# Longer rows for the tiles that hold the softplus's two halves

## The chip, the cores and the metric

One core of a Trainium2 chip runs the whole program. The metric is the time of one execution on the device, in microseconds. Before the change it is 933.11 us, the median of three runs (931.77 to 933.13).

## The reference

Three stages follow each other: a recurrence over time with complex decay (attention), a feed-forward network with softplus, and a gated one without a nonlinearity.

```python
# attention, per batch and head; a is scaled to a magnitude of at most 0.999
S_re, S_im = a_re*S_re - a_im*S_im + outer(k_t, v_t), a_re*S_im + a_im*S_re
y_t = q_t @ S_re                                    # 4 x 8 heads, 768 steps, 48 wide
x = y as (3072 tokens, 384)
h = x @ w_in;  g = max(h, 0) + log1p(exp(-abs(h)))  # 384 -> 2048, softplus
x = g @ w_out                                       # 2048 -> 384
out = ((x @ w1) * (x @ w2)) @ w3 @ w_out2           # 384 -> 1024 -> 1024 -> 384
```

## The kernel before

Attention is worked in 24 chunks of 128 steps: cumulative products of the decays by a scan on VectorE (tiles P and tm), then matmuls on scaled queries and keys (tiles qkp, pk, rs, sc, am, kT, S, yp). The first network takes the 3072 tokens in blocks: 128 and 256 tokens in plain float32 (tiles x, s, g, w), then seven blocks of 384. Those seven use pairs of float32r tiles, a rounded high half and the rest as a low half, and three products: high by high, low weight by high, high weight by low. For every group of 128 of the 2048 hidden columns (16 groups, index f) the function s1 makes nine matmuls into a PSUM tile s (weights ww..h and ww..l, moving operand xh or xl), three activations on ScalarE and one VectorE operation give the softplus g, ScalarE rounds it into gh (line 946), and VectorE subtracts, gl = g - gh (line 947). The function s2a then makes nine matmuls into three accumulators acc (moving operand gh or gl). The second network follows in six blocks of 512 tokens and eight groups: s3 makes 18 matmuls into pa and pb (moving operand in the tiles called bx: for even blocks in the slots of tag P, named bxh and bxl, for odd blocks in wb6 and wb7, shown as bx), VectorE and ScalarE make the product bg and its halves bgg (in the slots of xh and xl), and s2b makes nine matmuls into acc with the weights bwp.

On chip memory is laid out by pools, one behind the other in each of the 128 partitions, and in a pool by tag, in the order of first use; every tag has some slots, each one row long. Pool cp: identity and mask (512 bytes a row) and six small tiles. Pool wp: the weights, rows of 3072 or 6144 bytes. Pool sp: gh and gl (five slots of 1536 bytes each), e (two), xl and xh (two of 4608 each) and g (three of 1536). Pool ap: rs0, rs1 (8192), kT (3584), a, nt (3072), P (two of 6144), n2, tm, qk, qkp, v (480 floats, 1920 bytes), am, S and y. The first two gh slots hold ext at the start, two slots of gl hold pick: constants for attention, cleared by POOL (lines 576 to 583) and, for pick, filled from the identity by ten copies.

The order of all instructions is planned by the program itself: operations are recorded with prices (line 162 for POOL: `return 160 + n * 2.08, 200`, with n the elements a partition), and the method flush lists them by priority in 16 rounds, a backward and a forward pass each, of which the second adds random noise to the priorities (line 336); the round with the earliest end is kept. Operations that one wait links are found by 64-element cells of tiles. All DMAs are issued from SP's queue. Every recorded operation is shown with line 205, since there it is called.

Of the kernel before, what the change touches and what calls it, by code (L numbers as in the profile page):

```python
# [11 lines left out]
F32 = mybir.dt.float32  # L12
F32R = mybir.dt.float32r
# [9 lines left out]
P = 128  # L23
# [11 lines left out]
NB = 384  # L35

BLOCKS = [(0, 128), (128, 256)] + [(NB * i, NB) for i in range(1, NT // NB)]
NATIVE = 2
QKB = 1
GB = 3  # L40
HB = 5
# [319 lines left out]
def fused(ctx: ExitStack, tc: tile.TileContext, a_in, qk_in, v_in, wio, w12, w3t, wo2, q, k, v, a_re, a_im, outT):  # L361
# [18 lines left out]
    sp = fast.enter_context(tc.tile_pool(name="sp", bufs=2))  # L380
# [42 lines left out]
    def pst(tag, bufs, shape, name):  # L423
        return ps.tile(shape, F32, tag=tag, bufs=bufs, name=name)
# [29 lines left out]
    def norm(u):  # L454
# [27 lines left out]
        def s4():  # L482
# [9 lines left out]
            )  # L492

        return [s1, s2, s3, s4]

    def cmul(R, L):
# [68 lines left out]
    def qkp(u, i, f):  # L565
        V.tensor_tensor(
            out=c[u]["qkp"][:, :, :, i],
            in0=half(u),
            in1=gt(f).unsqueeze(1).to_broadcast([P, 2, G, T]),
            op=ALU.mult,  # L570
        )
# [1 line left out]
    def vcols(h):  # L573
        return slice(h * 64, h * 64 + D) if h < 6 else slice(384 + (h - 6) * D, 384 + (h - 5) * D)

    ext = [sp.tile([P, NB], F32, tag="gh", bufs=HB, name=f"ext{i}") for i in range(2)]
    for t in ext:
        GP.memset(t, 0.0)
    ext = [t.rearrange("p (r k n) -> p r k n", r=2, k=KC) for t in ext]
    picks = [sp.tile([P, NB], F32, tag="gl", bufs=HB, name=f"pick{i}") for i in range(2)]  # L580
    sels = {}
    for i in range(2):
        GP.memset(picks[i], 0.0)
    for h in range(H):
        for g in range(h * D // P, ((h + 1) * D - 1) // P + 1):
            p0 = max(h * D, g * P)
            n = min((h + 1) * D, (g + 1) * P) - p0
            i, c0 = divmod(len(sels) * 64, NB)
# [11 lines left out]
    def inv(u):  # L600
# [14 lines left out]
        def s3():  # L615
            s["qkp"] = ap.tile([P, 2, G, 2, T], F32, tag="qkp", bufs=QKB, name=f"qkp{u}")
            qkp(u, 0, s["qk"][:, 0])
# [35 lines left out]
        if u < PICK:  # L653
            return [s1, s2, s3, lambda: pick(0), s4, s5, lambda: pick(1)]
        return [s1, s2, s3, s4, s5, s6]

    def mm(u):
# [88 lines left out]
        def x():  # L746
            bi, c0 = block_of(u)
            if c0 == 0:
                if bi < NATIVE:
                    xt[bi] = (sp.tile([P, KC, NB], F32, tag="xh", bufs=XB, name=f"x{bi}"), None)  # L750
# [5 lines left out]
            xh, xl = xt[bi]  # L756
            if bi < NATIVE:
                A.copy(xh[:, :, d], s["y"][:, 0:KC])
# [18 lines left out]
    for us in groups:  # L777
        n = len(us)
# [131 lines left out]
    def w_split(f):  # L910
        ww[f] = w_tiles(f, f"ww{f}")
        split(ww[f][0], ww[f][1], w32[f])
# [3 lines left out]
    def s1(bi, f):  # L916
        _, n = BLOCKS[bi]
        native = bi < NATIVE
        if bi == NATIVE:
            w_split(f)  # L920
        xh, xl = xt[bi]
        pt = pst("s1", S1B, [P, NB], f"s1_{bi}_{f}")
        o = pt[:, 0:n]
        if native:
            prods = [(w32[f], xh)]
        else:
            prods = [(ww[f][0], xh), (ww[f][1], xh), (ww[f][0], xl)]
        i = 0
        for w, xx in prods:
            for k in range(KC):  # L930
                PE.matmul(
                    o, w[:, k * P : (k + 1) * P], xx[:, k, 0:n],
                    start=(i == 0), stop=(i == len(prods) * KC - 1),
                )
                i += 1
        e = sp.tile([P, NB], F32, tag="e", name=f"e_{bi}_{f}")[:, 0:n]
        A.activation(out=e, in_=o, func=AF.Abs)
        A.activation(out=e, in_=e, func=AF.Exp, scale=-1.0)
        A.activation(out=e, in_=e, func=AF.Ln, bias=1.0)
        g = sp.tile([P, NB], F32, tag="g", bufs=GB, name=f"g_{bi}_{f}")[:, 0:n]  # L940
        V.scalar_tensor_tensor(out=g, in0=o, scalar=0.0, in1=e, op0=ALU.max, op1=ALU.add)
        if native:
            return g, None
        gh = sp.tile([P, NB], F32R, tag="gh", bufs=HB, name=f"gh_{bi}_{f}")[:, 0:n]
        gl = sp.tile([P, NB], F32R, tag="gl", bufs=HB, name=f"gl_{bi}_{f}")[:, 0:n]
        A.copy(gh, g)
        V.tensor_tensor(out=gl, in0=g, in1=gh.bitcast(F32), op=ALU.subtract)
        return gh, gl
# [12 lines left out]
    def s2a(bi, f, gg):  # L961
        _, n = BLOCKS[bi]
        gh, gl = gg
        if bi < NATIVE:
            prods = [(w32[f][:, DM:], gh)]
# [58 lines left out]
    for bi in range(nblk):  # L1024
        last = bi == nblk - 1
        t0, n = BLOCKS[bi]
# [89 lines left out]
    for bi in range(NBB):  # L1116
        gq = {}
        for f in range(FB):
# [6 lines left out]
            while ncheck[0] < min(NCK, NCK * it // nit):  # L1125
                src, n = cks[ncheck[0]]
# [11 lines left out]
    for src, lim, op in (  # L1138
# [5 lines left out]
        n = src.shape[1]  # L1144
# [249 lines left out]
```

## Time and profile before

| | |
|---|---|
| median of three runs | 933.11 us |
| profiled execution | 932.9 us |
| its span, first to last instruction | 931.2 us |
| TensorE, matmuls busy | 905.4 us, 97% |
| VectorE busy | 727.6 us, 78% |
| ScalarE busy | 540.6 us, 58% |
| POOL busy | 12.2 us, 1% |
| mean granted TensorE clock | 0.998 |

Times in the profile count from the first instruction. Busy is the time in which an engine has an instruction; a matmul's duration overlaps with the next one's, so what a matmul costs is the distance between two starts. A plain float32 matmul has two records, a float32r matmul one. The names are those of the program, out<-in, buffer numbers left out; of a matmul's two inputs the first is the moving operand, the second the weights.

### The profile page before, as it was taken

Reading aid. Unit: us, or ns where it says so; the run is one execution under the profiler, and the core shown is the slowest. Engines: PE = TensorE matmul, PEld = TensorE weight load, DVE = VectorE, ACT = ScalarE, POOL = GpSimd, SP = SyncE. Lnnn points to the kernel's source line nnn. Section 1 sums busy time; section 2 is a strip of 40 time slices with the busy share of each in tenths; the row PEclk is TensorE's granted clock in tenths of the full one; section 3 lists DMA queues with packets and bytes.
Section 4 is the critical chain, followed back from the end, with each engine's and each line's share of the span. In section 5 each row is a group of like instructions: output and inputs, shape, how many; then the busy total and the mean of one; then the engine's idle time right before and its main releaser. Section 6 shows DMA issues by size and latency. Waiting matters only on the chain.

```text
span 931.2 us, 16377 instructions
## 1 busy us (share of the span) xinstructions
PE 905.4 (97%) x6081; PEld 815.5 (88%) x6081; DVE 727.6 (78%) x1591; ACT 540.6 (58%) x1111; POOL 12.2 (1%) x29
## 2 busy tenths in 40 slices
PE   3999999999999999999999999999999999999997
PEld 2579988899999999999999999998888888888885
DVE  6999999999999899999989855599888785231221
ACT  6679986478597688778676755773231323131212
POOL 5000000000000000000000000000000000000000
PEclk9999999999999999999999999999999999999999
DMA  9898218375444737363746255248888873000001
GB/s 341 302 329 311 67 49 197 94 161 132 124 116 115 191 65 183 86 167 62 204 117 154 77 135 140 68 145 247 248 261 246 255 239 120 1 34 0 35 1 38
DMA packets 81641, 136.38 MB, mean 146 GB/s; under 512 B 7504, under 2 KB 53136, under 8 KB 81552
## 3 DMA queue, kind: packets, MB, share of 16 engines
q1 hardware_dynamic: 81552, 135.25, 50.4%
q8 instruction: 49, 0.80, 0.4%
q14 instruction: 40, 0.33, 0.1%
HBM read 107.59 MB, written 26.74 MB: 144 GB/s over the span
## 4 chain that ended last, share of the span: by engine, by line
PE 81%; DVE 11%; DMA 4%; issue 1%; ACT 1%; SPq 1%; DVEq 0%; ACTq 0%
PE acc L205 28%; PE s L205 17%; PE pb L205 11%; PE pa L205 11%; PE yp L205 4%; PE wpa L205 3%; PE sc L205 3%; DVE tm L205 3%; DVE P L205 3%; DMA a<-a_in 2%; PE stp L205 1%; PE pk L205 1%; PE ktp L205 1%; DVE g L205 1%; DVE qkp L205 1%
## 5 line engine op out<-in xcount | busy, mean ns | idle before, releaser
L205 DVE TENSOR_TENSOR tm<-P 128x90 f32<-128x90 f32 (+3 forms) x240 | 145.9, 619 | 1.3
L205 ACT ACTIVATE e<-e 128x384 f32<-128x384 f32 (+2 forms) x288 | 134.6, 487 | 2.2
L205 DVE TENSOR_TENSOR bg<-pa,bg 128x512 f32<-128x512 f32 x48 | 33.1, 689 | 92.6 <-PE pa L205 82.3
L205 ACT ACTIVATE e<-s 128x384 f32<-128x384 f32 (+2 forms) x144 | 64.7, 452 | 59.6 <-PE s L205 51.4
L205 ACT CAST bgg<-bg 128x512 fp32r<-128x512 f32 x48 | 29.8, 621 | 104.2 <-DVE bg L205 104.2
L205 DVE SCALAR_TENSOR_TENSOR g<-s,e 128x384 f32<-128x384 f32 (+2 forms) x144 | 73.4, 514 | 17.4 <-ACT e L205 16.3
L205 DVE TENSOR_TENSOR P<-tm 128x45 f32<-128x45 f32 (+11 forms) x304 | 85.7, 345 | 1.0
L205 ACT COPY bg<-pb 128x512 f32<-128x512 f32 x48 | 28.2, 588 | 88.0 <-PE pb L205 79.3
L205 ACT CAST gh<-g 128x384 fp32r<-128x384 f32 x112 | 56.6, 507 | 17.2 <-DVE g L205 15.0
L205 DVE TENSOR_TENSOR gl<-g,gh 128x384 fp32r<-128x384 f32 x112 | 61.7, 557 | 5.2 <-ACT gh L205 4.9
L205 PE MATMUL wpa<-wo,w 128*128 128x384 f32 x128 | 44.6, 509 | 14.2 <-DVE w L205 14.2
L205 DVE CUSTOM_DVE_ANT_0 ck<-ckr 128x384 f32<-128x384 f32 x80 | 43.4, 543 | 16.2 <-DMA ckr<-w3t 7.0
L205 PE MATMUL sc<-rs 112*128 112x128 f32 x384 | 52.2, 276 | 0.7 <-DVE am L205 0.6
L205 PEld LDWEIGHTS wpa<-wo,w 128*128 128x128 f32 x128 | 25.2, 200 | 31.6 <-DVE w L205 14.1
L205 PEld LDWEIGHTS sc<-rs 112*128 112x128 f32 x384 | 49.6, 191 | 2.7 <-DVE g L205 0.9
L205 PE MATMUL acc<-bgg,bwp0h 128*128 128x512 f32 x144 | 50.4, 389 | 0.0
L205 PE MATMUL acc<-bgg,bwp2h 128*128 128x512 f32 x144 | 48.7, 389 | 0.0
L205 DVE TENSOR_TENSOR bgg<-bg,bgg 128x512 fp32r<-128x512 f32 x48 | 33.0, 688 | 15.8 <-ACT bgg L205 15.8
L205 DVE TENSOR_REDUCE lims<-ck 128x1 f32<-128x384 f32 x80 | 43.1, 539 | 2.3
L205 PE MATMUL yp<-am,v 128*48 128x128 f32 (+1 forms) x360 | 40.9, 277 | 0.0
L205 PE MATMUL acc<-g,w 128*128 128x128 f32 (+1 forms) x192 | 38.5, 331 | 0.0
L205 DVE TENSOR_TENSOR am<-sc,mask 128x512 f32<-128x512 f32 x48 | 33.5, 697 | 6.4 <-PE sc L205 5.7
(386 smaller groups left out, 2405.0 us busy)
## 6 DMA issues: line engine op xcount, KB each, us to landing
pd<-qkp SPq DMA_DIRECT2D x20, 768.0 KB, 4.5
rs<-pd SPq DMA_DIRECT2D x40, 384.0 KB, 6.3
ckr<-wio SPq DMA_DIRECT2D x32, 384.0 KB, 3.8
wr<-wio SPq DMA_DIRECT2D x32, 383.8 KB, 7.0
a<-a_in SPq DMA_DIRECT2D x24, 384.0 KB, 3.4
qk<-qk_in SPq DMA_DIRECT2D x24, 384.0 KB, 4.0
w12r<-w SPq DMA_DIRECT2D x16, 384.0 KB, 3.5
ckr<-w SPq DMA_DIRECT2D x16, 384.0 KB, 3.7
```

The lines of the kernel that those rows point to most:

```text
L205: getattr(engine.unit, op)(*args, **kw)
```

## The change

A row of the tiles with tags gh and gl gets 400 elements in place of 384, and what is used of it stays its first 384 (or n) elements. For ext and for the softplus's halves the slice is taken at once; the tiles pick are kept whole, so that they are cleared over 400 columns. Every slot behind the first of gh so begins 64 bytes further than the one before it would, and everything behind the ten slots 640 bytes further. Instructions, their number and their operands' shapes are otherwise the same.

```diff
--- before.py
+++ after.py
@@ -36,6 +36,7 @@
 
 BLOCKS = [(0, 128), (128, 256)] + [(NB * i, NB) for i in range(1, NT // NB)]
 NATIVE = 2
+GW = NB + 16
 QKB = 1
 GB = 3
 HB = 5
@@ -573,11 +574,11 @@
     def vcols(h):
         return slice(h * 64, h * 64 + D) if h < 6 else slice(384 + (h - 6) * D, 384 + (h - 5) * D)
 
-    ext = [sp.tile([P, NB], F32, tag="gh", bufs=HB, name=f"ext{i}") for i in range(2)]
+    ext = [sp.tile([P, GW], F32, tag="gh", bufs=HB, name=f"ext{i}")[:, 0:NB] for i in range(2)]
     for t in ext:
         GP.memset(t, 0.0)
     ext = [t.rearrange("p (r k n) -> p r k n", r=2, k=KC) for t in ext]
-    picks = [sp.tile([P, NB], F32, tag="gl", bufs=HB, name=f"pick{i}") for i in range(2)]
+    picks = [sp.tile([P, GW], F32, tag="gl", bufs=HB, name=f"pick{i}") for i in range(2)]
     sels = {}
     for i in range(2):
         GP.memset(picks[i], 0.0)
@@ -941,8 +942,8 @@
         V.scalar_tensor_tensor(out=g, in0=o, scalar=0.0, in1=e, op0=ALU.max, op1=ALU.add)
         if native:
             return g, None
-        gh = sp.tile([P, NB], F32R, tag="gh", bufs=HB, name=f"gh_{bi}_{f}")[:, 0:n]
-        gl = sp.tile([P, NB], F32R, tag="gl", bufs=HB, name=f"gl_{bi}_{f}")[:, 0:n]
+        gh = sp.tile([P, GW], F32R, tag="gh", bufs=HB, name=f"gh_{bi}_{f}")[:, 0:n]
+        gl = sp.tile([P, GW], F32R, tag="gl", bufs=HB, name=f"gl_{bi}_{f}")[:, 0:n]
         A.copy(gh, g)
         V.tensor_tensor(out=gl, in0=g, in1=gh.bitcast(F32), op=ALU.subtract)
         return gh, gl
```

## Rows read from the trace of the kernel before

**Rows 1.** The page: span, and busy time of each engine with its share.
```profile
span 931.2 us, 16377 instructions
...
PE 905.4 (97%) x6081; PEld 815.5 (88%) x6081; DVE 727.6 (78%) x1591; ACT 540.6 (58%) x1111; POOL 12.2 (1%) x29
```

**Rows 2.** Stretches in us: busy (count) of PE, PEld, DVE, ACT, POOL; clock, DMA, GB/s.
```profile
100.00:200.00 100.00, 97.88 (x832) 88.87 (x829) 96.59 (x222) 72.69 (x168) 0.00 (x0) 1.00 0.46 115
200.00:300.00 100.00, 100.00 (x835) 98.25 (x834) 99.11 (x222) 76.64 (x165) 0.00 (x0) 1.00 0.51 125
300.00:400.00 100.00, 98.41 (x789) 95.30 (x788) 94.21 (x210) 76.06 (x164) 0.00 (x0) 1.00 0.54 134
400.00:500.00 100.00, 99.78 (x756) 97.09 (x755) 93.32 (x206) 76.11 (x169) 0.00 (x0) 1.00 0.53 129
500.00:600.00 100.00, 99.53 (x754) 97.73 (x753) 64.32 (x131) 62.46 (x131) 0.00 (x0) 1.00 0.45 117
740.00:800.00 60.00, 60.00 (x266) 49.68 (x265) 37.82 (x98) 14.42 (x23) 0.00 (x0) 1.00 0.50 157
```

**Rows 3.** The page: the chain that ended last, by engine and by line.
```profile
PE 81%; DVE 11%; DMA 4%; issue 1%; ACT 1%; SPq 1%; DVEq 0%; ACTq 0%
PE acc L205 28%; PE s L205 17%; PE pb L205 11%; PE pa L205 11%; PE yp L205 4%; PE wpa L205 3%; PE sc L205 3%; DVE tm L205 3%; DVE P L205 3%; DMA a<-a_in 2%; PE stp L205 1%; PE pk L205 1%; PE ktp L205 1%; DVE g L205 1%; DVE qkp L205 1%
```

**Rows 4.** The chain in order of time: start us, us, what, how many matmul records.
```profile
128.41 3.45 PE s L205 x16
...
215.61 2.60 PE s L205 x15
...
334.34 2.60 PE acc L205 x15
...
737.38 2.04 PE acc L205 x9
```

**Rows 5.** Timeline of TensorE, 501 to 503 us: start us, us, instruction, count.
```profile
501.51 0.39 PE L205 MATMUL yp<-am,v 128*48 128x128 f32 x4
...
502.83 0.39 PE L205 MATMUL yp<-am,v 128*48 128x128 f32 x4
503.05 0.35 PE L205 MATMUL stp<-v,kT 128*64 128x48 f32 x7
```

**Rows 6.** VectorE's groups by form: out<-in, shapes, count | busy us, mean ns.
```profile
L205 DVE TENSOR_TENSOR gl<-g,gh 128x384 fp32r<-128x384 f32 x112 | 61.7, 557 | 5.2 <-ACT gh L205 4.9
...
L205 DVE TENSOR_TENSOR am<-sc,mask 128x512 f32<-128x512 f32 x48 | 33.5, 697 | 6.4 <-PE sc L205 5.7
...
L205 DVE TENSOR_TENSOR bgg<-bg,bgg 128x512 fp32r<-128x512 f32 x48 | 33.0, 688 | 15.8 <-ACT bgg L205 15.8
...
L205 DVE TENSOR_TENSOR xl<-y,xh 128x384 fp32r<-128x384 f32 x18 | 10.1, 558 | 0.5 <-ACT xh L205 0.4
```

**Rows 7.** ScalarE's groups by form.
```profile
L205 ACT CAST gh<-g 128x384 fp32r<-128x384 f32 x112 | 56.6, 507 | 17.2 <-DVE g L205 15.0 <-PE acc L205 1.8
...
L205 ACT CAST xh<-y 128x384 fp32r<-128x384 f32 x18 | 9.2, 512 | 4.8 <-DMA y<-y 4.1 <-ACT nt L205 0.6
```

**Rows 8.** Timeline of POOL, 0 to 16 us.
```profile
6.68 0.74 POOL L205 MEMSET wtop_wa<- 128x768 int32 x1
7.36 0.78 POOL L205 MEMSET pick<- 128x384 f32 x2
...
12.07 0.77 POOL L205 MEMSET ext<- 128x384 f32 x2
```

**Rows 9.** Tile pk, its matmuls: duration ns min/median/max, first and last start in us.
```profile
L205 PE MATMUL pk<-qkp,pick x320: 272/273/324, 52.8 to 122.1; 128*64 128x128 f32 x160
```

**Rows 10.** Stretch 500 to 640 us for the tiles gh, gl and s, in this order.
```profile
500.00:640.00 140.00, 56.93 (x235) 41.69 (x234) 20.32 (x37) 17.66 (x35) 1.00 0.47 129
...
500.00:640.00 140.00, 36.55 (x120) 21.91 (x119) 20.32 (x37) 1.00 0.47 129
...
500.00:640.00 140.00, 57.68 (x288) 50.28 (x288) 18.63 (x35) 16.02 (x33) 1.00 0.47 129
```

## The prediction

> **What bounds the kernel now.** I read the shares of the page first, then the table by stretches, then the shares of the chain, then its pieces. The profiled execution took 932.9 us, 931.2 us of it span and 1.7 us around it; the median of the three timed runs is 933.11, 0.2 us above, so a sum made on the trace needs no correction. TensorE is busy for 905.4 of 931.2 us [rows 1]. From 100 us on it hardly stops: in the stretches from 100 to 500 us it is idle for 2.12 + 0 + 1.59 + 0.22 = 3.9 us in all, at full granted clock, and VectorE is idle for 3.41 + 0.89 + 5.79 + 6.68 = 16.8 us of the same 400; from 500 us on VectorE has a third free and TensorE still none [rows 2]. The chain that ended last runs through matmuls: those of line 205's acc, s, pb and pa alone hold 67% of it, VectorE's tm and P 6% [rows 3]. So a change is worth what it does to the spacing of matmuls, and before 500 us also what it does to VectorE.
>
> What a matmul takes is read from the chain's pieces, length over count [rows 4]. The float32r matmuls (three products of high and low halves) of 384 columns follow each other every 2.60/15 = 173.3 ns in s and in acc, those of 512 columns every 2.04/9 = 226.7 ns. At 2.4 GHz their columns alone are 160.0 and 213.3 ns, so each has 13.3 ns on top, whatever its length. A plain float32 record of 256 columns (two records are one matmul, at two clocks a column) takes 3.45/16 = 215.6 ns, 2.3 ns over its columns.
>
> **The change part by part.** Rows of all tiles in the pools wp, sp and ap ahead of v are whole multiples of 512 bytes (3072, 6144, 1536, 4608, 8192, 3584), so today gh, gl, g, e, xh, xl, rs, P and the weights all begin at the same place modulo 512: in step. The v row (480 floats) is 1920 bytes; am, S and y behind it begin 384 bytes out of step, and the mask and the identity of the first pool 288 bytes before the step.
>
> *The matmuls that read moved operands.* With ten rows of 1600 bytes, the five gh tiles stand 0 to 256 bytes out of step with the weights, the five gl tiles 320, 384, 448, 0 and 64, and all later tiles 640, which is 128. By the loops these are, in seven blocks with 16 steps of 9 each: 1008 matmuls into acc (gh, gl), 1008 into s (xh, xl, moved by 128); in the second network 432 into acc (their bgg lies in xh and xl), and of the 864 into pa and pb the 432 of even blocks, whose operand lies in P; odd blocks read wb6 and wb7, which stay. In sum 2880 of the 3312 float32r matmuls change their place against the weights. No instruction is added for them; the cost is 2880 times whatever the place does to the spacing.
>
> The trace has no float32r matmul out of step, so I take it from the nearest rows, and these are good ones. In the output of a head's pair, S is read as weights at 192 bytes a head from a base 384 off, while rs, the moving operand, is in step: over eight heads that gives 384, 64, 256, 448, 128, 320, 0 and 192, every multiple of 64 there is, and v and am alternate with them at 128, 320 or 384. From 501.51 to 503.05 us seven groups of four such records take 1.54 us, 0.22 each, and the last of them 0.22 again [rows 5]. With the reading of two decimals that binds the effect of any of the eight places on a float32 record of 128 columns to 0.01/4 = 2.5 ns, either way. They read half as fast as float32r, which is why this is a bound and not a proof. I take 0, the value of the row, and keep 3 ns either way: 2880 x 3 = 8.6 us, so 924 to 942.
>
> *VectorE and ScalarE on moved tiles.* The subtraction of 128x384 with both inputs and its output in step (gl from g and gh) takes 557 ns; the same with one input 384 out of step (xl from y and xh) takes 558. Of 512 columns, the product with all in step (bgg) takes 688 ns, the one with mask and am out of step 697 [rows 6]. ScalarE's cast takes 507 ns in step (gh from g) and 512 from y [rows 7]. I take 0; the ends are 9 ns on 112 gl, 1.0 us, and 5 ns on 112 gh, 0.6 us, and those lie only half in the stretches where VectorE is full. In the other direction 1 ns on 112, 0.1 us. DMAs keep their number, sizes and order on SP's queue, and their addresses move by multiples of 64 bytes; I take 0 for them too. They hold 4% of the chain [rows 3], so it would take a twentieth on each of those to pass 1.9 us.
>
> *Two memsets.* The tiles ext are cut back to 384 columns before they are cleared, the tiles pick are cleared whole, 400 columns. The clears of 768 columns take 0.74 us and two of 384 take 0.78 [rows 8], so a column is about (740 - 390)/384 = 0.9 ns, 16 more in two clears 29 ns. POOL is done at 12.84 us, and the first matmul that reads pick starts at 52.8 us [rows 9]: hidden under 40 us. No wait is added and no queue is passed; nothing stands behind those clears on POOL but ten copies and the clears of ext, which have the same 40 us.
>
> *The order.* The kernel plans its own order from prices, and a memset's price is 160 + 2.08 ns a column: the two go from 958.7 to 992.0. Nothing on another engine waits for POOL within those 40 us, and slices, slots and 64-element cells of all other tiles stay. So each engine's order should stay as it is.
>
> Sum: 0 + 0 + 0 + 0 on 932.9, or 933.0 beside the median.
>
> **The rivals.**
>
> *The 13.3 ns are collisions of the weight load with the moving read, and being in step causes them (faster).* For it: the surplus is the same at 384 and 512 columns, as a cost per weight load would be, and float32 at half the read rate has only 2.3. Out of step it would sink towards 2.3, 11 ns for each of 2880, 31.7 us. But of the 2016 matmuls of the first network 235 + 120 + 288 = 643 are behind 500 us [rows 10]; the gain of the 1373 before them (15.1 us) has to fit into VectorE's 16.8 us of idle time in the same stretches, which is scattered, and I let half through, 7.5; behind 500 us 643 + 864 matmuls give 16.6. That is 24 us, 909. If only 2.5 ns go, the resolution of rows 5, it is 7 us, 926. Against it: two operands that advance at unlike speeds should pass through all places whatever their first one; the eight places of rows 5 cost the same; and between 200 and 300 us, with VectorE 99% busy in the same memory, the spacing is the 173.3 ns of any other stretch.
>
> [...]
>
> *New collisions (slower).* Today all float32r streams have one phase, and they run with a spread of nothing. If it is this phase that is free of a clash between the moving row and the weight load that runs beside it, the ten phases of gh and gl and the one of xh, xl and bgg lose it. Place: acc and s from 140 us on; price: up to the 3 ns above, 8.6 us, 942, paid in full because TensorE has no idle time to take it. It decides from 0.65 ns a matmul (1.9 us over 2880). Against it: rows 5 again.
>
> *The order changes after all (either sign).* One of the planner's 16 rounds adds noise to the operations in the order of their backward starts, where six POOL operations come 33 ns later. If one passes a neighbour, all later rounds differ. In the plan of the kernel before, worked out by its own prices, none does, the closest by 2 ns. Price: TensorE's idle time from 100 to 500 us, 3.9 us, lost or paid once more: 929 to 937.
>
> **How the numbers follow.** I call within 0.2% (1.9 us) no change: the three runs before spread over 1.36 us, 0.15%. Forecast 0.74, between 931.2 and 935.0. Collisions gone 0.13, half of it near 909 and half near 926. New collisions 0.09. Other order 0.04, of it a quarter faster, a quarter the same, half slower. So faster 0.14, same 0.75, slower 0.11. The range takes the forecast and both ends of the 3 ns: 924 to 942; outside it lie the large gain and a sliver of the loss, under 0.1.
>
> **What would show it.** Right: acc and s of 384 columns again 173.3 ns apart and those of 512 again 226.7, odd and even blocks of pa and pb alike; gl 557 and gh 507 ns; TensorE's 905 us; the same order on every engine; the two clears of pick some 29 ns longer. The odd blocks are the control inside the changed kernel: if even blocks run at another spacing than odd ones, the place matters. Wrong: a spacing of gh's matmuls that differs from tile to tile, or an order that differs from the first rows on.

## The result, and the profile after

The changed kernel takes 940.66 us, the median of three runs (939.03 to 941.03), against 933.11 before: a ratio of 1.0081 with a 95% interval of 1.0058 to 1.0104. It is slower by 7.6 us. The profiled execution has a span of 939.2 us, 8.0 more than before [rows 1].

The order of the instructions is the same on every engine, so pieces of the same name and count at the same point of the two chains are the same matmuls. From the page of the changed kernel:

```profile
span 939.2 us, 16377 instructions
...
PE 913.7 (97%) x6081; PEld 818.0 (87%) x6081; DVE 728.1 (78%) x1591; ACT 540.9 (58%) x1111; POOL 13.0 (1%) x29
...
PE 85%; DVE 6%; DMA 4%; ACT 1%; SPq 1%; issue 1%; DVEq 0%; ACTq 0%
```

TensorE's busy time grew by 8.3 us, that of VectorE and ScalarE by 0.5 and 0.3. TensorE's granted clock is 0.999 for 0.998 and its idle time 25.5 us for 25.8. The matmuls themselves take longer. Pieces of the chain in order of time (start us, us, what, count) of the changed kernel:

```profile
215.93 2.64 PE s L206 x15
...
334.57 2.60 PE acc L206 x15
...
637.52 2.32 PE pa L206 x10
...
692.47 2.05 PE pb L206 x9
...
733.15 2.10 PE acc L206 x9
...
767.94 2.10 PE pb L206 x9
...
926.13 6.08 PE acc L206 x26
```

and five more of the kernel before, the same matmuls as the last five above, beside [rows 4]:

```profile
635.61 2.27 PE pa L205 x10
...
689.33 2.04 PE pb L205 x9
...
729.45 2.04 PE acc L205 x9
...
762.99 2.04 PE pb L205 x9
...
918.26 5.91 PE acc L205 x26
```

Fifteen matmuls of 384 columns that took 2.60 us take 2.64 (176.0 ns each) or still 2.60. Nine of 512 columns that took 2.04 us take 2.10 (233.3) where all operands moved (733.15, bgg; 767.94, pb of an even block), and 2.05 (227.8) in one piece of an odd block, whose own moving operand did not; a hundredth of a us more is within the reading of one piece. From the piece of s to the last piece the loss can be placed: from 215.61 to 635.61 before and from 215.93 to 637.52 after, 420.00 against 421.59, is 1.6 us in the first network; from pa to the last acc, 282.65 against 288.61, is 6.0 us in the second. So some three quarters lie in the third of the time that has 512 columns.

From the starts of all matmuls of the second network, the mean distance to the next one goes from 226.7 to 232.1 ns in acc, from 226.8 to 232.6 in pa and pb of even blocks and from 226.7 to 229.1 in odd ones. Over 432 each that is 2.3, 2.5 and 1.0 us, together 5.8 of the 6.0. In the odd blocks the cost is a matter of order: right behind a matmul whose operand moved, the first five take 229.4 to 233.0 ns in the mean, and from the tenth in a row on they take 226.7 again, as before. A stretch of TensorE's timeline in the changed kernel (start us, us, instruction, count) has such a run, its first three 0.70 us and the next three 0.68:

```profile
692.08 0.39 PE L206 MATMUL acc<-bgg,bwp0l 128*128 128x512 f32 x1
692.30 0.86 PE L206 MATMUL pb<-bx,bw2h 128*128 128x512 f32 x3
693.00 0.84 PE L206 MATMUL pb<-bx,bw2l 128*128 128x512 f32 x3
693.68 0.84 PE L206 MATMUL pb<-bx,bw2h 128*128 128x512 f32 x3
```

VectorE and ScalarE on the moved halves (groups by form, as [rows 6, 7]):

```profile
L206 DVE TENSOR_TENSOR gl<-g,gh 128x384 fp32r<-128x384 f32 x112 | 61.4, 554 | 5.3 <-ACT gh L206 4.9
```

```profile
L206 ACT CAST gh<-g 128x384 fp32r<-128x384 f32 x112 | 56.6, 507 | 17.9 <-DVE g L206 15.7 <-PE acc L206 1.9
```

554 for 557, 507 for 507. And POOL's timeline, as [rows 8]: the two clears of pick take 0.80 us for 0.78, and POOL ends at 13.67 us, still 39 us ahead of the first matmul that reads pick.

```profile
7.36 0.80 POOL L206 MEMSET pick<- 128x400 f32 x2
...
12.90 0.77 POOL L206 MEMSET ext<- 128x384 f32 x2
```

### The profile page after: what moved, and what is told of

It reads as the page before. It is cut to its first block, busy times and chain, and to the rows that moved or that the text cites. A ratio compares the mean times of both kernels' runs of the same rounds, so it can differ in the third digit from the quotient of the medians.

```text
span 939.2 us, 16377 instructions
## 1 busy us (share of the span) xinstructions
PE 913.7 (97%) x6081; PEld 818.0 (87%) x6081; DVE 728.1 (78%) x1591; ACT 540.9 (58%) x1111; POOL 13.0 (1%) x29
## 4 chain that ended last, share of the span: by engine, by line
PE 85%; DVE 6%; DMA 4%; ACT 1%; SPq 1%; issue 1%; DVEq 0%; ACTq 0%
PE acc L206 31%; PE s L206 20%; PE pb L206 11%; PE pa L206 11%; PE yp L206 4%; PE sc L206 4%; PE wpa L206 2%; DMA wr<-wio 2%; PE stp L206 2%; DVE tm L206 2%; DVE P L206 2%; DMA a<-a_in 2%; PE ktp L206 1%; PE pk L206 1%; SPq L206 1%; DMA w3r<-w3t 1%
## 5 line engine op out<-in xcount | busy, mean ns | idle before, releaser
L206 DVE SCALAR_TENSOR_TENSOR g<-s,e 128x384 f32<-128x384 f32 (+2 forms) x144 | 73.0, 511 | 16.7 <-ACT e L206 15.6
```

The costliest lines, as they stand in the source:

```text
L206: getattr(engine.unit, op)(*args, **kw)
```

## The experiments

In what follows "place" is where a moving operand begins, in bytes behind the place of the weights. A spacing of a stream is worked out from the starts of its last 49 matmuls; a row of the timeline, (length less the last one's 0.39 or 0.33 us)/59, takes in the stream's first matmuls and gives up to 1 ns more. Each stream kernel ran once. Where a gap is put in, POOL clears it by one more instruction at the start; the order of everything else on the four engines is that of the kernel before.

**Matmuls alone.** 60 at a time, weights cycling through 12 column groups, nothing beside them (the code of the three stream kernels is shortened here):

```diff
+for n in (512, 384):
+    for s in PHASES:     # 0, 16, 32, 48, 64, 96, 128, 192, 256, 320, 384, 448, 512, 640
+        for i in range(60):
+            matmul(o[:, 0:n], wr[:, (i % 12) * 128:][:, 0:128], mv[s][:, 512 * (i % 3):][:, 0:n])
```

> This kernel leaves the whole computation out: it streams float32r matmuls, 60 of a kind, whose moving operand begins 0 to 640 bytes out of step with the weights (modulo 512), with no work on any other engine beside them; 512 and then 384 columns; three stretches at the end of each alternate between two places. Theory A (the place of the moving operand against the weights sets the spacing of matmuls, with nothing else needed): 226.7 and 173.3 ns at 0 and at 512, which is in step again; about 232.4 and 175 ns at 128 and at 640; the other places each their own, between 224 and 241 ns. Theory B (the place brings matmuls into conflict with what VectorE, ScalarE or DMAs do at the new addresses): 226.7 and 173.3 ns everywhere, since nothing runs beside.

The timeline of TensorE in this kernel (start us, us, instruction, count; m128x is the operand at place 128), 512 columns and then 384:

```profile
102.94 14.16 PE L48 MATMUL o<-m128x,wr 128*128 128x512 f32 x60
...
130.94 13.78 PE L48 MATMUL o<-m256x,wr 128*128 128x512 f32 x60
144.56 13.91 PE L48 MATMUL o<-m320x,wr 128*128 128x512 f32 x60
...
186.26 13.78 PE L48 MATMUL o<-m512x,wr 128*128 128x512 f32 x60
...
255.22 10.56 PE L48 MATMUL o<-m0x,wr 128*128 128x384 f32 x60
...
318.05 10.72 PE L48 MATMUL o<-m128x,wr 128*128 128x384 f32 x60
```

Theory A holds and B falls: with no other engine at work, 512 columns at place 128 are 233.3 ns apart and at 512 226.7; 384 columns 176.1 and 173.3. These distances are also of the size of the loss in the whole kernel: 6.6 ns on the 864 matmuls of the second network that moved are 5.7 us, beside 6.0 measured there. New is that 256 is as good as 0, and 320 as 64 (both 228.9). With the two later stream kernels the list is, in ns (512 columns / 384 columns):

| place | spacing | place | spacing | place | spacing |
|---|---|---|---|---|---|
| 0, 256, 512 | 226.7 / 173.3 | 64, 320 | 228.9 / 173.3 | 160 | 234.3 / 176.7 |
| 4 | 238.6 | 80 | 231.1 / 173.3 | 176 | 233.3 / 176.1 |
| 8 | 233.3 | 96 | 233.3 / 176.7 | 192, 448 | 233.3 / 174.6, 176.7 |
| 16, 272 | 231.7 / 175.6 (at 16) | 112 | 226.7 / 173.3 | 208 | 234.7 / 176.7 |
| 32 | 233.3 / 173.3 | 128, 384, 640 | 232.4 to 233.3 / 175.9 to 176.1 | 224 | 233.3 |
| 48 | 233.3 / 175.0 | 144 | 233.3 / 174.7 | 240 | 226.6 or 233.3 / 180.0 |

For 512 and 384 columns no place tried is better than the one that the kernel before has; place 112 is as good. The single distances are not alike: in step they read 226 or 227 ns throughout, at 128 bytes 238 and 229 by turns or, in a later stream at the same place, 228 to 241 in a longer pattern. Streams that alternate between 0 and 128 settle at 230.0, half way.

**The halves alone.** Only gh's rows are longer, gl begins at place 320, and a gap brings all later tiles back in step:

```diff
+GW = NB + 16
...
-    ext = [sp.tile([P, NB], F32, tag="gh", bufs=HB, name=f"ext{i}") for i in range(2)]
+    ext = [sp.tile([P, GW], F32, tag="gh", bufs=HB, name=f"ext{i}")[:, 0:NB] for i in range(2)]
...
+    gap = sp.tile([P, 48], F32, tag="gap", bufs=1, name="gap")
+    nc.gpsimd.memset(gap, 0.0)
...
-        gh = sp.tile([P, NB], F32R, tag="gh", bufs=HB, name=f"gh_{bi}_{f}")[:, 0:n]
+        gh = sp.tile([P, GW], F32R, tag="gh", bufs=HB, name=f"gh_{bi}_{f}")[:, 0:n]
```

> Only gh and gl out of step (gh 0 to 256 bytes by slot, gl 320), all later tiles back in step by a gap of 192 bytes. Theory A: the second network is as before (226.7 ns), the first loses what its acc lost in the changed kernel, at most 1 to 2 us: 933 to 935. Theory C (the change costs where gh and gl are written and read, in VectorE and ScalarE): all 7.6 us, 940.

933.26 us beside 932.59 for the kernel before on the same chip, ratio 1.0008 (0.9998 to 1.0018): no change that can be told, and by the interval at most 1.7 us. Its chain:

```profile
216.35 2.61 PE s L206 x15
...
636.34 2.27 PE pa L206 x10
...
730.18 2.04 PE acc L206 x9
...
919.36 5.91 PE acc L206 x26
```

The second network is back at 2.04/9 = 226.7 ns. The first takes 636.34 - 216.35 = 419.99 us, as before. So the tiles that the change names cost nothing that can be told, gh at its five places and gl at one of its five. By the streams of 384 columns it would be some 0.5 us (gh at places 0, 64, 128, 192 and 256), too little for this comparison.

**The later tiles alone.** gh and gl as before, and a gap behind them:

```diff
+    gap = sp.tile([P, 32], F32, tag="gap", bufs=1, name="gap")     # 128 bytes
+    nc.gpsimd.memset(gap, 0.0)
     sels = {}
```

> gh and gl in step as before, a gap of 128 bytes behind them, so that only the later tiles (e, xl, xh, g, and all of the attention's) are 128 bytes out of step. Theory A: bgg and the even blocks of pa and pb at about 232 ns as in the changed kernel, s at 174 to 175: 6 to 7 us of the loss, 939 to 940. Theory C: 933.

940.36 us, ratio 1.0082 (1.0066 to 1.0098): the whole loss, without one longer row. The chain is that of the changed kernel:

```profile
215.64 2.64 PE s L205 x15
...
638.11 2.33 PE pa L205 x10
...
733.78 2.10 PE acc L205 x9
...
768.17 2.10 PE pb L205 x9
...
926.34 6.08 PE acc L205 x26
```

Of its loss 422.47 - 420.00 = 2.5 us are in the first network and 288.23 - 282.65 = 5.6 in the second. Theory C falls. Theory A gave 6 to 7 us of loss and s at 174 to 175 ns; it is 7.8 us, and this piece of s runs at 2.64/15 = 176.0.

**Everything moved.** The same 128 bytes ahead of the weights, so that weights and operands move together:

```diff
+    gap = cp.tile([P, 32], F32, name="gap")
+    nc.gpsimd.memset(gap, 0.0)
     NCK = 2 * FA + 6 * FB
```

> A gap of 128 bytes ahead of the weights: every tile of the networks moves by 128 bytes, weights too, so the addresses of the later tiles are those of later_only while moving operands and weights stay in step. Theory A: no change, 933, spacing 226.7 and 173.3. Theory D (the absolute address counts, a row's start against some boundary): as later_only, 939 to 940.

933.19 us, ratio 1.0006 (0.9996 to 1.0016). The later tiles stand at the addresses of later_only, and the spacing is that of before:

```profile
690.07 2.05 PE pb L205 x9
...
730.21 2.04 PE acc L205 x9
...
919.77 5.91 PE acc L205 x26
```

Theory D falls: it is the place against the weights.

**A gap of 256 bytes, and one of 32.** As the later tiles alone, with 64 and with 8 elements in the gap (against the kernel of the later tiles alone):

```diff
-    gap = sp.tile([P, 32], F32, tag="gap", bufs=1, name="gap")
+    gap = sp.tile([P, 64], F32, tag="gap", bufs=1, name="gap")     # 256 bytes; in the other run [P, 8], 32 bytes
```

> As later_only, with a gap of 256 bytes in place of 128. By the streams (period of 256 bytes): spacing 226.7 and 173.3 again, 933, no change. If in step had to mean modulo 512: some 232 ns, 939 to 940.

933.44 us, ratio 1.0005 (0.9994 to 1.0016). In its chain:

```profile
346.08 5.75 PE s L205 x33
...
730.09 2.04 PE acc L205 x9
...
763.64 2.04 PE pb L205 x9
```

In step means modulo 256 in the whole kernel too.

> As later_only, with a gap of 32 bytes. By the streams 384 columns stay at 173.3 ns there and 512 go to 233.3: the first network as before, bgg and the even blocks slower by some 6 ns, 938 to 940. If the place counted alike for both lengths: the first network would lose too.

939.71 us, ratio 1.0070 (1.0052 to 1.0088). In its chain:

```profile
214.20 2.60 PE s L205 x15
...
345.62 5.84 PE s L205 x33
...
635.23 2.33 PE pa L205 x10
...
731.35 2.10 PE acc L205 x9
...
924.81 6.08 PE acc L205 x26
```

The second network loses 289.58 - 282.65 = 6.9 us, the first 421.03 - 420.00 = 1.0 where later_only lost 2.5. That the first would lose nothing was not right: some pieces of s run at 2.60/15 = 173.3 ns as the stream at this place does, others do not (5.84 for 33 against 5.75). That piece of 33 follows matmuls of the attention and repeats 174, 178, 175 and 180 ns to its end, so here too one place has two spacings.

**What takes part in it.** Streams with fewer weight columns, with moved weights, of fewer moving columns, with one group of weights throughout, at more places (in the table above), and in plain float32:

```diff
+for cols in (128, 96, 64, 32):        # 60 matmuls each, place 0 and 128
+    matmul(o[0:cols, 0:n], wr[:, j * P : j * P + cols], mv[s][...])
...
+run(mv[0], ws); run(mv[128], ws)      # ws: the weights, 128 bytes later
...
+run(f0, w, n=256); run(f128, w, n=256)  # plain float32
```

> This kernel leaves the whole computation out: streams of 60 matmuls as in the first stream kernel, 512 columns where nothing is said. Theory A1 (the surplus over the columns' own time is the weight load's reads getting in the way of the moving operand's, and the place decides how often): with 96, 64 and 32 weight columns the 13.3 ns at place 0 and the 20.1 ns at place 128 shrink in step, to about 10, 6.7 and 3.3, and 15, 10 and 5; with the weights themselves moved by 128 the two places change roles (233.4 at 0, 226.7 at 128); places 4 and 8, 224 and 240 between 226 and 235; 272 as 16, 231.6; plain float32 of 256 columns 215.6 a record at both places. Theory A2 (the address of the moving operand alone decides, the weight load has no part): 226.7 and 233.4 at any number of weight columns, and the same with moved weights.

```profile
46.71 13.98 PE L53 MATMUL o<-m0x,wr 128*96 128x512 f32 x60
60.53 14.05 PE L53 MATMUL o<-m128x,wr 128*96 128x512 f32 x60
...
102.10 14.05 PE L53 MATMUL o<-m0x,wr 128*32 128x512 f32 x60
115.99 14.00 PE L53 MATMUL o<-m128x,wr 128*32 128x512 f32 x60
129.83 14.10 PE L53 MATMUL o<-m0x,wshift 128*128 128x512 f32 x60
143.77 13.82 PE L53 MATMUL o<-m128x,wshift 128*128 128x512 f32 x60
...
227.22 7.36 PE L53 MATMUL o<-m0x,wr 128*128 128x256 f32 x60
234.41 7.29 PE L53 MATMUL o<-m128x,wr 128*128 128x256 f32 x60
...
282.55 13.11 PE L53 MATMUL o<-f0x,wraw 128*128 128x256 f32 x60
295.50 13.11 PE L53 MATMUL o<-f128x,wraw 128*128 128x256 f32 x60
```

The weights' place counts as much as the operand's: moved weights turn the two places round (232.5 at 0, 226.7 at 128), so A2 falls. But A1 falls as well. Fewer weight columns do not shrink the surplus: 230.0 ns with 96 and with 64, 231.7 with 32, where 223 or less was expected at place 0. But they do take most of the effect of the place away: at place 128 it is 231.7, 231.1 and 230.8 ns with 96, 64 and 32, so the 6.6 ns between the two places with 128 weight columns shrink to 1.7, 1.1 and -0.9. The number of moving columns counts too. With 256 place 128 is no worse than place 0 (118.8 and 120.0 ns), and with 128 both take 111.7. One group of weights throughout gives 226.7 and 233.3 as twelve do. Plain float32 is 215.8 ns a record at either place. Place 4, at 238.6, is outside the 226 to 235 that were expected.

**Own weights or the next ones.** Two streams that alternate operand and weights:

```diff
+run([(mv[0], wr), (mv[128], ws)])     # in step with its own weights, not with the next one's
+run([(mv[0], ws), (mv[128], wr)])     # the other way round
...
+run([(mv[0], wr)], n=500)             # and 480, 448
```

> This kernel leaves the whole computation out: streams of 60 float32r matmuls again. Two streams alternate moving operands at 0 and 128 bytes with weights at 0 and 128. In the first each matmul is in step with its own weights and out of step with the next one's, in the second the other way round. Theory A3 (what counts is the moving operand against the weights that are loaded beside it, the next matmul's): first about 233, second 226.7 ns. Theory A4 (against its own weights): first 226.7, second 233. If the spacing comes in steps of 6.67 ns, which 226.7 = 34, 173.3 = 26 and 120.0 = 18 of them and 512, 384 and 256 columns = 32, 24 and 16 suggest, 480 and 448 columns in step give 32 and 30 steps, 213.3 and 200.0, and 500 columns a mean that is no whole number of steps, near 222 to 227. If a fixed cost of 13.3 ns is added to the columns instead: 213.3, 200.0 and 221.7. Places 80 to 240 at 512 and 384 columns: none under 226.7 and 173.3 if in step is the best there is.

228.3 ns for the first and 230.0 for the second: neither A3 nor A4. 480 columns in step take 216.7 ns, 448 take 202.7 and 500 take 223.3, so neither a fixed 13.3 ns nor whole steps of 6.67 hold for these lengths. None of the new places is under 226.7 and 173.3. Place 240 gave 233.3 here, behind a stream at 208, and 226.6 in the stream kernel ahead of this one, behind one at 224. That the stream ahead decides this was not tried by itself; the operand also lay in another slot.

## Why the prediction was wrong

- *The sum's main term, 2880 matmuls times what the place does.* I set it to 0; it measures 7.6 us over them, 2.6 ns each, near the end of 3 ns that I had kept, which is why 940.66 lies inside the range. That is luck: the 3 ns were the reading of a row of another kind of matmul and no bound on this kind, of which one of 512 columns at place 128 loses 6.6 ns. The step that failed is the transfer from [rows 5]. Those records differ from the matmuls that the change moves in more than the half read rate that I named and passed over (by [rows 5] 0.22/2 = 0.11 us for 128 columns, 0.86 ns each, beside 226.7/512 = 0.44 in float32r): they are plain float32, have 128 columns and 48 weight columns, and run two at a time, with starts some 7, 104, 8 and 101 ns apart, so that even their own bound is 0.01/2 = 5 ns and not 2.5. The streams find no effect of the place in plain float32 of 256 columns (215.8 ns at both), none in float32r of 128 columns (111.7), and little in float32r with few weight columns. Which of the differences hid it in [rows 5] stays open.
- *The rival that came true* is the one with 0.09, new collisions, priced at up to 8.6 us. That TensorE would pay, having no idle time, was right. Its place was not: I put it into acc and s from 140 us on; by halves_only, acc with gh and gl pays nothing that can be told, and some three quarters are in the second network.
- *The counts.* The 2880 hold some 340 of gh and gl that do not move or move by a whole 256 bytes: by the prediction's own places, one slot in five of each stays in step, and one gh slot in five stands at 256. I held the 432 matmuls of odd blocks for untouched and proposed them as a control. They slow down too, from 226.7 to 229.1 ns in the mean, since they follow matmuls whose operand moved; only from the tenth in a row on do they run as forecast. So a control inside the changed kernel was not clean.
- *The rival "collisions gone"* had its sign from the surplus of 13.3 ns. The columns' own time that it leaves out is what the rows give: (226.7 - 173.3)/128 = 0.417 ns a column between 384 and 512 columns of float32r, and twice that in plain float32, (322.5 - 215.6)/128 = 0.835 ns between records of 256 columns (s) and of 384 (wpa, 322 or 323 ns from start to start in the kernel before). For 512 and 384 columns the surplus is there at the best of the places tried, so leaving the step had nothing to give back. Nor is it the same at every length, as the prediction had it: in step it is 13.3 ns at 512, 384 and 256 columns, but 15.0 at 500, 16.7 at 480 and 16.0 at 448. Plain float32 of 256 columns has 2.5 ns in the streams (215.8 a record), float32r 12.1 ns or more in each. In the stream kernels, with every other engine still, moving one operand by 128 bytes costs 6.6 ns a matmul of 512 columns (233.3 for 226.7); what in the hardware takes them no run shows.
- *VectorE, ScalarE, POOL and the order* came out as written: 554 and 507 ns for 557 and 507, two clears 20 ns longer (29 forecast) under 39 us of cover, the same order on all engines.
- *The point that should have warned me:* a spread of nothing, 226 or 227 ns in nearly every matmul of 512 columns. The prediction names it, as the premise of "new collisions" (one phase, perhaps the one that is free of a clash), and then lets [rows 5] outweigh it. It was the sign that all float32r streams stood at one and the same place, and that no other place was on record for them.

## What to carry to other kernels

Where matmuls run back to back, an added byte ahead of a pool moves every later tile; look what stands behind the tile that is changed, for here that was the whole loss. A resource that shows one value only, without spread, has been measured at one point: bound it by a stream of its own before setting it to zero. For float32r of 384 and 512 columns with 128 weight columns it pays to keep moving operands and weights in step modulo 256 bytes (226.7 and 173.3 ns, beside 233.3 and 176.1 at place 128), and no place tried was better; with 256 columns (118.8 ns at place 128, 120.0 in step) and 128 (111.7 at both), or with 96, 64 or 32 weight columns (1.7, 1.1 and -0.9 ns between the two places), the streams show little or nothing to be had, at place 128, the only other one tried there.

## What the runs showed of the hardware

The spacing of float32r matmuls with 128 weight columns depends on where the moving operand begins against the weights: 226.6 to 238.6 ns for 512 columns, 173.3 to 180.0 for 384. Places 256 bytes apart (0 and 256, 16 and 272, 64 and 320, 128 and 384, 192 and 448) agree to 1 ns for 512 columns and, without 272, to some 2 ns for 384. With 96, 64 or 32 weight columns places 0 and 128 differ by 1.7 ns or less. Out of step the distances follow a pattern of some matmuls that repeats, as 238 and 229 ns by turns. What came before counts too: behind matmuls out of step, matmuls in step take up to 233.0 ns in the mean and need some nine to get back to 226.7, and one place can have two spacings (32 bytes: 173.3 or 176.7 ns for 384 columns). Shown is that place, weights and history of the stream take part; by what mechanism stays open. Of the ideas that I proposed, the weight load's reads as the source of the whole surplus, own or next weights' place alone, and whole steps of 6.67 ns all fell in the form in which I put them; the weight load may still have a part, since with narrower weights places 0 and 128 come out nearly alike.
